# Expert results as blocks in a table by slot, gathered per token, and transposes ahead of the second small output

## The chip, the cores and the metric

The kernel runs on one core of a Trainium2 chip. The metric is the time of one execution in microseconds, as the device measures it. The kernel before takes 564.56 us (median of three runs, 564.34 to 565.74).

## The reference

Three layers follow one another, all in float32. An attention whose queries are averaged in pairs gives 1152 tokens of 512 numbers. A mixture of eight experts then adds to each token the gated result of one expert, unless a score of the token says that it is passed on unchanged. A feed-forward of width 2048 ends it.

```python
def _moe_ref(x, w_skip, w_gate, w1, w2):
    do_compute = x @ w_skip > 0
    out = x.copy()
    xc = x[do_compute]
    logits = xc @ w_gate
    e_idx = np.argmax(logits, axis=1)
    probs = softmax(logits)                       # 1e-9 added to the sum
    gate_w = probs[np.arange(len(xc)), e_idx]
    for e in range(E):                            # E = 8
        mask = e_idx == e
        h = np.maximum(xc[mask] @ w1[e], 0.0)     # 512 -> 1024
        y[mask] = gate_w[mask, None] * (h @ w2[e])
    out[do_compute] = xc + y
    return out

def _moe2_ref(x, w_in, w_out):
    h = x @ w_in                                  # 512 -> 2048
    return (h * np.tanh(softplus(h))) @ w_out     # 2048 -> 512
```

## The kernel before

The core works in three stages, and the program order on each engine is written out by hand (`manual_schedule`), so an engine takes its instructions in the order of the code.

**Attention** (to about 231 us) leaves the tokens in the DRAM tensor `rows` (1152 x 512). Beside it SyncE fills `ytok`, a DRAM tensor of the same shape, with zeros, three blocks of 128 rows at each of the steps 13, 16 and 19 (`early`, L1326 to L1329), loads expert weights and prepares the weights of the feed-forward.

**Routing** (`routing`, L484) counts with matrix products which token goes to which expert and place. Each expert has first 32 places ("small"); experts 0 and 2 have 256 and 128 places more and, like the others, a tail of 64 ("mid"). The result is `idx`, for each place the number of its token, in columns of 128 places; `sidx` is the same list with a number out of range for places without a token, and `odd` a copy of part of it. Tokens are gathered from `rows` through `idx` by GpSimd's indirect DMAs (`fetch`, L633).

**Experts** (`moe`, L879). `small1` and `small2` compute up and down projection for the 32 places of an expert; four experts share the rows of one tile `ys[0]` or `ys[1]`. `wide` (L717) treats the larger places of experts 0 and 2, with operands that are split in a high and a low part. The order at the beginning is: `turn` of the small hidden values of expert 0, the transposes `prep0(0)`, `turn` for expert 1, `small2(0)`, `prep0(1)`, the subtraction `wlo(0, 2)`, `small2(1)`, `prep0(2)`, and then `wide(0)`. `prep0(j)` transposes the j-th tile of expert 0's tokens into PSUM; ScalarE copies the high part out (L714) and VectorE subtracts for the low part (L715). `small2` sums its two halves with an `L801` copy on ScalarE and two adds on VectorE (L804); its PSUM tile has the tag "ys", with one buffer, except for the last expert, which uses "yl".

Every result is scattered into `ytok` by token with an indirect DMA on GpSimd's queue (`put`, L691; places without a token fall out of range). There are six before the feed-forward's first third: three after `wide(0)`, one for `ys[0]`, two after `wide(2)`. Then GpSimd loads the first 384 rows of `ytok` into `yt` (L979). VectorE adds them, times the gate, to the tokens (L990), while TensorE goes through the small experts 4 to 7. The result of these, `ys[1]`, is scattered last (L995); for the first third of the tokens it is added not by way of `ytok` but by a matrix product with the selection `pick` (L1126).

**Feed-forward** (`ffn`, L1088). `prep_first` transposes the first third (L1119) and adds the product with `pick` (L1126). Then 48 steps follow, 16 for each third of the tokens. At the fifth step of the first and second third, SyncE and ScalarE load the next third of `rows` and `ytok` (`load_x`, L1105), and `add_x` (L1109) adds them from the eighth step on.

Behind it stands a conditional part (`others`, and a second feed-forward) for inputs with more tokens at an expert than the places hold. It doesn't run with these inputs.

Of the kernel before, what the change touches and what calls it, by code (L numbers as in the profile page):

```python
# [17 lines left out]
N = B * Q  # L18
# [9 lines left out]
MID = 64  # L28
TAIL = 2 + E * (S // P)
NCOL = TAIL + E // 2  # L30
ZROW = NCOL * P
# [4 lines left out]
NEAR = slice(2, 2 + len(ROWS))  # L36
TAILS = slice(NEAR.stop - E // 2, NEAR.stop)
# [446 lines left out]
def routing(tc, io, lg, rt, tmp, ps, first, second, third, kept):  # L484
# [42 lines left out]
    count = rk[:, T * E :]  # L527
    sidx, idx, cnt, odd = kept
    pr = te("r_pr")
# [20 lines left out]
    def tokens(cs, ix):  # L550
        nc.vector.tensor_scalar(idx[:, cs], ix, float(FAR), float(N - 1), op0=ALU.add, op1=ALU.min)
        return lambda: nc.vector.tensor_scalar(sidx[:, cs], ix, float(FAR), None, op0=ALU.add)
# [18 lines left out]
    nc.vector.tensor_reduce(f, pos, axis=AX.X, op=ALU.add)  # L571
    fi = sb([P, T], I32, "r_fi")
    nc.vector.tensor_scalar(fi, f, float(ZROW), None, op0=ALU.add)
# [55 lines left out]

    return dict(idx=idx, sidx=sidx, odd=odd, cnt=cnt, gates=gates)  # L630

# [38 lines left out]


def source(io, e, i):
    if i < 2:
        src = io["w1"][e, 2 * P * i : 2 * P * i + 2 * P]
    else:
        src = io["w2"][e, 4 * P * (i - 2) : 4 * P * (i - 1)]
    return src.rearrange("(k p) f -> p k f", p=P)


def passes(nc, tc, io, r, rows, ytok, wts, ps, wk, nreg, xs, wait=None):  # L680
    idx, cnt = r["idx"], r["cnt"]
    gather = lambda dst, col: fetch(nc, rows, idx, dst, col)

    def scatter(src, col, n=P, odd=0):
        if odd:
            ix = r["odd"][:, col - TAILS.start : col - TAILS.start + 1]
        else:
            ix = r["sidx"][:n, col : col + 1]
        put(src, ix)
# [27 lines left out]
    def wide(e, xT, w1, split, outs, hooks):  # L717
        J = DEEP[e]
        n = P * J + MID
        two = len(w1) == 2  # L720
        acc = [ps.tile([P, 512], F32, name="ly", tag="yl")]
        acc += [ps.tile([P, 512], F32, name="lt", tag="mt", bufs=2) for _ in range(J)]
        gs = {}

        def hidden(fc):
            a = ps.tile([P, 512], F32, name="la", tag="am", bufs=2)[:, :n]
            prods = [(k, i) for k in range(4) for i in (PASS if two else ((0, 0),))]
            for m, (k, (u, v)) in enumerate(prods):
                nc.tensor.matmul(  # L729
                    a, w1[u][k // 2][:, k % 2, P * fc : P * fc + P], xT[v][:, k, :n],  # L730
                    start=(m == 0), stop=(m == len(prods) - 1),
                )
            g = [wk.tile([P, 5 * MID], F32R, name=x, tag=x)[:, :n] for x in ("wh", "wl")]
            nc.scalar.activation(g[0], a, AF.Relu)  # L734
            nc.vector.scalar_tensor_tensor(g[1], a, 0.0, g[0].bitcast(F32), op0=ALU.max, op1=ALU.subtract)  # L735
            gs[fc] = g

        def outp(fc):
            g = gs.pop(fc)
            for j in range(J + 1):  # L740
# [67 lines left out]
    def mid(e, xm, fill):  # L808
# [13 lines left out]
        down(MID, turn(MID, hs, "m", hT[:, :4]), (wts[e, 2], wts[e, 3]), yo, "l")  # L822
        scatter(yo, COL[e - e % 2, None], MID, e % 2)

    def large(e, j, xg, xgT):
# [21 lines left out]
        nc.scalar.copy(xg, y)  # L847
        scatter(xg, COL[e, j])

# [11 lines left out]
    def rest(e, xm, xg, end, before=None):  # L861
# [11 lines left out]
    return dict(  # L873
        gather=gather, scatter=scatter, put=put, register=register, transp=transp, turn=turn,
        down=down, larges=larges, rest=rest, prep=prep, wide=wide,
    )


def moe(tc, io, r, rows, ytok, slot, early, xr, yg, ylast, pick, last, xsT, ps, xm0, hs0, wts, whi, wlo):  # L879
    nc = tc.nc  # L880
    with ExitStack() as ctx:
# [4 lines left out]
        p = passes(nc, tc, io, r, rows, ytok, wts, ps, wk, {}, ())  # L886
        gather, scatter, turn, down = (p[n] for n in ("gather", "scatter", "turn", "down"))

# [77 lines left out]
        def last3():  # L966
            small2(3, hs[3])
            load_w(24, 30)
            scatter(ys[0], 0)

# [23 lines left out]
        small2(E - 1, hT, "l")  # L994
        p["put"](ys[1], last)  # L995


def others(tc, io, r, rows, ytok):
    nc = tc.nc
    with ExitStack() as ctx:  # L1000
        pool = lambda name, bufs, **k: ctx.enter_context(
# [86 lines left out]
def ffn(tc, io, r, rows, ytok, wdec, out, xr, yg, ylast, pick, wi, first, late=lambda: None):  # L1088
    nc = tc.nc
    T = 9  # L1090
    with ExitStack() as ctx:
# [204 lines left out]
def body(tc, io, out):  # L1296
    nc = tc.nc
    with ExitStack() as ctx:
# [20 lines left out]
        pick = cp.tile([P, 3, P], F32, name="pick")  # L1319
        last = cp.tile([P, 1], I32, name="last")  # L1320
        zero = cp.tile([P, DM], F32, name="zero")
# [4 lines left out]
        def early(i):  # L1326
            if i < 3:
                for t in range(3 * i, 3 * i + 3):
                    nc.sync.dma_start(ytok[P * t : P * t + P], zero)  # L1329
# [12 lines left out]
            cp.tile(x, I32, name=n)  # L1342
            for n, x in (("sidx", [P, NCOL]), ("idx", [P, NCOL]), ("cnt", [P, 2 * E + 1]), ("odd", [MID, E // 2]))
        ]
        kp = pool("kp", 1)

# [11 lines left out]
        with ExitStack() as c2:  # L1358
# [54 lines left out]
            r["gate"] = gate  # L1413
            moe(tc, io, r, rows, ytok, slot, split, xr, yg, zero, pick, last, xsT, ps, xm0, hs0, wts, whi, wlo)
        most = []

        def ask():
            most.append(
                nc.values_load(
                    kept[2][0:1, 2 * E : 2 * E + 1], min_val=-N, max_val=N,  # L1420
                    skip_runtime_bounds_check_because="a count of tokens",
# [4 lines left out]
        with tc.If(most[0] > SMALL):  # L1426
            others(tc, io, r, rows, ytok)
            again = Split(nc, kp)
            again.wdec = wdec
            again.open(8)  # L1430
            ffn(tc, io, r, rows, ytok, wdec, out, xr, yg, zero, pick, again, False)

# [4 lines left out]
def layout(inp):  # L1437
# [19 lines left out]
    cst[:, CST["iota"]] = ar  # L1457
    ids = [0, 1] + [TAIL + e // 2 if j is None else 2 + S // P * e + j for e, j in ROWS]
    cst[:, CST["c128"]] = np.array(ids) * P
# [4 lines left out]
    cst[:, CST["base"]] = SMALL * e8 - ZROW  # L1464
    cst[:, CST["lofs"]] = (S - SMALL) * e8 + 2 * P - SMALL
    cst[:, CST["tofs"]] = (MID - S) * e8 + (TAIL - 2) * P
    res = dict(
# [33 lines left out]
```

## Time and profile before

| | us |
|---|---|
| median of three runs (564.34 to 565.74) | 564.56 |
| the profiled execution, as a whole | 565.0 |
| its span, first to last instruction | 563.2 |
| TensorE busy (96% of the span) | 538.0 |
| VectorE busy (69%) | 388.2 |
| ScalarE busy (66%) | 372.2 |
| GpSimd busy (17%) | 96.9 |

The profile is of one execution; its times run from the first instruction of the span. A row of a view names the line of the kernel, the engine (PE is TensorE, DVE VectorE, ACT ScalarE, POOL GpSimd, SP SyncE; PEld is the load of weights into TensorE, beside its products), the operation and the tensors as output<-input. Busy time isn't progress: an engine with 96% can still have its holes at one place, so the stages are looked at one by one. A DMA that is issued from GpSimd shows as a short instruction of GpSimd, and its landing comes later.

### The profile page before, as it was taken

How to read it: one execution, taken by the hardware profiler on the slowest of the kernel's cores; microseconds unless marked ns; L12 is line 12 of the kernel's file. 1: busy time of each engine (PE TensorE's matmuls, PEld its weight loads, DVE VectorE, ACT ScalarE, POOL GpSimd, SP SyncE). 2: the span in 40 equal slices, each digit the busy share in tenths (PEclk: the TensorE clock that was granted, in tenths of full speed). 3: DMA queues.
4: the chain of work that ended last, by engine and by line, in shares of the span. 5: the costliest groups of instructions: out<-in, count | busy, mean ns of one | idle time of the engine just before them, and what ended most of it. 6: DMA issues, size and time to landing. Idle time of an engine off the chain costs nothing. (4 is left out here: it accounts for less than half of the span.)

```text
span 563.2 us, 11886 instructions
## 1 busy us (share of the span) xinstructions
PE 538.0 (96%) x4770; PEld 411.5 (73%) x4772; DVE 388.2 (69%) x725; ACT 372.2 (66%) x677; POOL 96.9 (17%) x88
## 2 busy tenths in 40 slices
PE   8699999999999999998999997999999999999994
PEld 4566666666666766657868746898899899999882
DVE  3488788888989888684133224899986666666663
ACT  3888888888888888632141141999877666676662
POOL 1213444335524511140000110000000000000000
PEclk9999999999999999998999998999999999999998
DMA  8558878998878783159979764273203100010001
GB/s 260 209 200 276 274 254 277 312 319 283 289 241 300 243 297 129 48 191 397 357 278 365 275 229 152 77 261 94 60 16 124 45 1 0 2 58 0 2 0 62
DMA packets 49922, 102.18 MB, mean 181 GB/s; under 512 B 13995, under 2 KB 15403, under 8 KB 49856
## 3 DMA queue, kind: packets, MB, share of 16 engines
q1 hardware_dynamic: 47360, 95.20, 49.2%
q0 software_dynamic: 1264, 3.75, 2.0%
q10 hardware_dynamic: 1232, 2.36, 1.2%
q8 instruction: 39, 0.64, 0.5%
q14 instruction: 27, 0.22, 0.1%
HBM read 84.70 MB, written 17.04 MB: 181 GB/s over the span
## 5 line engine op out<-in xcount | busy, mean ns | idle before, releaser
L152 DVE TENSOR_SCALAR_CACHE_REDUCE scp<-s 128x1152 f32<-128x1152 f32 x72 | 97.7, 1357 | 35.4 <-PE s L149 21.6
L1176 PE MATMUL ph<-xT,wi 128*128 128x384 f32 x576 | 108.5, 337 | 0.0
L1176 PEld LDWEIGHTS ph<-xT,wi 128*128 128x128 f32 x576 | 102.1, 188 | 4.2
L163 ACT ACTIVATE scp<-scp,mx 128x1152 f32<-128x1152 f32 x72 | 90.5, 1257 | 9.3 <-DVE scp L152 9.2
L149 PE MATMUL s<-ks,qs 64*128 64x288 f32 (+1 forms) x640 | 89.6, 428 | 5.2 <-DVE scp L152 4.8
L1230 PE MATMUL po<-wo,gh 128*128 128x512 f32 x288 | 90.3, 394 | 0.7 <-ACT gh L1215 0.5
L202 ACT COPY eT<-tp 128x1024 f32<-128x1024 f32 x63 | 63.8, 1013 | 27.6 <-PE tp L179 26.9
L149 PEld LDWEIGHTS s<-ks,qs 64*128 64x128 f32 (+1 forms) x640 | 48.9, 176 | 41.1 <-DVE scp L152 16.6
L220 PE MATMUL ov<-eT,vt 128*64 128x288 f32 x540 | 78.3, 417 | 0.0
L1230 PEld LDWEIGHTS po<-wo,gh 128*128 128x128 f32 x288 | 52.9, 188 | 10.2 <-ACT gh L1215 1.4
L1230 PE MATMUL po<-wo,gl 128*128 128x512 f32 x144 | 57.2, 397 | 0.0
L179 PEld LDWEIGHTS tp<-cst,scp 64*128 64x128 f32 x1145 | 47.0, 138 | 13.2 <-issue 3.9
L1200 ACT ACTIVATE u<-u 128x384 f32<-128x384 f32 (+1 forms) x49 | 25.4, 519 | 46.5 <-DVE u L1194 46.0
L1220 DVE TENSOR_TENSOR gl<-s,gh 128x384 fp32r<-128x384 f32 (+1 forms) x49 | 27.0, 550 | 41.7 <-ACT gh L1215 41.5
L351 POOL TENSOR_TENSOR g<-wd 128x512 f32<-128x512 f32 x32 | 34.0, 1063 | 89.0 <-PE s L149 74.7
L179 PE MATMUL tp<-cst,scp 64*128 64x64 f32 x1145 | 48.2, 223 | 0.0
L220 PEld LDWEIGHTS ov<-eT,vt 128*64 128x64 f32 x540 | 33.6, 136 | 19.2
L734 ACT ACTIVATE wh<-la 128x320 fp32r<-128x320 f32 (+1 forms) x16 | 6.2, 386 | 41.7 <-PE la L729 41.7
L735 DVE SCALAR_TENSOR_TENSOR wl<-la,wh 128x320 fp32r<-128x320 f32 (+1 forms) x16 | 6.8, 425 | 37.0 <-ACT wh L734 37.0
L1230 PEld LDWEIGHTS po<-wo,gl 128*128 128x128 f32 x144 | 27.0, 187 | 6.7 <-DVE gl L1220 1.0
L1194 DVE TENSOR_SCALAR u<-ph 128x384 f32<-128x384 f32 (+1 forms) x49 | 26.6, 545 | 6.4 <-PE ph L1176 6.3
L1202 ACT ACTIVATE r<-s,one 128x384 f32<-128x384 f32 (+1 forms) x49 | 30.0, 611 | 1.6
(195 smaller groups left out, 796.9 us busy)
## 6 DMA issues: line engine op xcount, KB each, us to landing
w<-w SPq DMA_DIRECT2D x32, 1024.0 KB, 8.7
wd<-wq SPq DMA_DIRECT2D x32, 512.0 KB, 5.5
wdec<-g SPq DMA_DIRECT2D x32, 256.0 KB, 4.6
vt<-vt SPq DMA_DIRECT2D x8, 576.0 KB, 5.7
ks<-kt SPq DMA_DIRECT2D x15, 288.0 KB, 6.8
ring<-wdec SPq DMA_DIRECT2D x16, 256.0 KB, 2.8
wr<-wdec SPq DMA_DIRECT2D x16, 256.0 KB, 2.7
xr<-qt SPq DMA_DIRECT2D x7, 576.0 KB, 6.1
```

Of the source, the lines that this page charges most:

```text
L149: st["tick"] = nc.tensor.matmul(s[o, half, j, :HQ], w[r], st["k", h, b][r, cs], start=True, stop=True).ins
L152: nc.vector.tensor_scalar(scp.rearrange("p (a c) -> p a c", a=4), s.rearrange("p a j c -> p (a j) c")[:, :, :HQ], -EXP_SCALE, -NEG, op0=AL ...
L163: nc.scalar.activation(scp, scp, AF.Exp, bias=mx, scale=-1.0, accum_out=st["sum", h][:, t : t + 1],)
L179: nc.tensor.matmul(to, e[q, P * i : P * i + P], io["ident"][q, q], start=i < 8 or a != opened, stop=True, is_transpose=True, skip_group_ch ...
L202: nc.scalar.copy(to.rearrange("p k (a c) -> p a k c", a=2), v)
L220: nc.tensor.matmul(acc[D * b : D * b + D, :288], st["v", h][:, b, kc], src[:, kc, b], start=(kc == 0), stop=(kc == KC - 1), skip_group_che ...
L351: side.append(lambda: tt(g, hf, hf, op=ALU.mult))
L1176: nc.tensor.matmul(ph, wi.w[i][:, a, P * k : P * k + P], xTs[c][b][:, k], start=(n == 0), stop=(n == 11),)
L1194: nc.vector.tensor_scalar(a["t"][0][:, c], ph[:, c], 20.0, None, op0=ALU.min)
L1202: nc.scalar.activation(r[:, c], s[:, c], AF.Ln, bias=one)
L1220: nc.vector.tensor_tensor(gl[:, c], a["t"][1][:, c], gh[:, c].bitcast(F32), op=ALU.subtract)
L1230: nc.tensor.matmul(acc[j], g[a][:, P * j : P * j + P], wo[b][:, i], start=(i == 0 and n == 0), stop=(i == 15 and n == 2),)
```

## The change

The table `ytok` is no longer by token but by place. Every block of places has fixed rows in it (`rowof`): the small places of experts 0 to 3 and 4 to 7 the first two blocks of 128 rows, then the tails, then the blocks of experts 0 and 2, and a block of zeros. A result is written as a block with a plain DMA on GpSimd's queue (`save`). Routing computes for each token the row that holds its result (`place`; a token without one points at the zeros), and the first third's load, as well as the two loads in the feed-forward, become three indirect gathers of 128 rows each on GpSimd's queue. The loads in the feed-forward were on ScalarE's queue. The lists `sidx`, `odd` and `last` go. Thirteen blocks are filled with zeros instead of nine, five, four and four at the same three steps. The conditional part gets a larger table of its own (`yall`), filled when it runs.

At the beginning of the experts, `prep0(1)` moves ahead of `small2(0)`, `prep0(2)` ahead of `wlo(0, 2)` and `small2(1)`, and `small2(1)` uses the PSUM tile "yl".

```diff
-TAIL = 2 + E * (S // P)
-NCOL = TAIL + E // 2
+TAIL = 2
+NCOL = TAIL + E // 2 + E * (S // P)
+FIRST = {e: TAIL + E // 2 + S // P * i for i, e in enumerate([*DEEP, *(e for e in range(E) if e not in DEEP)])}
+HEAD = max(FIRST[e] + DEEP[e] for e in DEEP)
...
-    slots = tokens(slice(0, 2), ix)
+    tokens(slice(0, 2), ix)
     first(idx)
+    nc.vector.tensor_scalar(spot, ix[:, 1:2], float(FAR), None, op0=ALU.add)
...
-    nears = tokens(NEAR, ix[:, NEAR])
+    tokens(NEAR, ix[:, NEAR])
+    nc.vector.tensor_scalar(near, f, float(ZROW), float(P * HEAD), op0=ALU.add, op1=ALU.min)
...
-    fars = tokens(far, ix[:, far])
-    for f in (slots, nears, fars):
-        f()
-    nc.vector.tensor_copy(odd, sidx[MID:, TAILS])
+    tokens(far, ix[:, far])
...
+def rowof(e, j):
+    if j is None:
+        return P * (TAIL + e // 2) + MID * (e % 2)
+    return P * (FIRST[e] + j)
...
-    def put(src, ix):
-        nc.gpsimd.indirect_dma_start(
-            out=ytok,
-            out_offset=bass.IndirectOffsetOnAxis(ap=ix, axis=0),
-            in_=src, in_offset=None, bounds_check=N - 1, oob_is_err=False,
-        )
+    def save(src, row):
+        nc.gpsimd.dma_start(ytok[row : row + src.shape[0]], src)
...
-            scatter(outs[j][:q], COL[e, j if j < J else None], q)
+            save(outs[j][:q], rowof(e, j if j < J else None))
...
-        nc.vector.tensor_copy(last, r["sidx"][:, 1:2])
-        spot = xp.tile([P, 1], F32, name="spot")
-        nc.vector.tensor_copy(spot, r["sidx"][:, 1:2])
...
         hT.append(turn(SMALL, hs0[1], "s", act=True))
+        prep0(1)
         small2(0, hT[0])
-        prep0(1)
+        prep0(2)
         wlo(0, 2)
-        small2(1, hT[1])
-        prep0(2)
+        small2(1, hT[1], "l")
         load_w(12, 20)
...
-            scatter(ys[0], 0)
+            save(ys[0], 0)
...
-        nc.gpsimd.dma_start(yt, tiles3(ytok, 0))
+        for t in range(3):
+            fetch(nc, ytok, r["place"], yt[:, t], t)
...
         small2(E - 1, hT, "l")
-        p["put"](ys[1], last)
+        save(ys[1], P)
...
         def load_x(c):
             nc.sync.dma_start(xr, tiles3(rows, c))
-            nc.scalar.dma_start(yg, tiles3(ytok, c))
+            for t in range(3):
+                fetch(nc, ytok, r["place"], yg[:, t], 3 * c + t)
...
-        ytok = dp.tile([N, DM], F32, name="ytok")
+        ytok = dp.tile([P * HEAD + P, DM], F32, name="ytok")
+        yall = dp.tile([ZROW + P, DM], F32, name="yall")
...
             if i < 3:
-                for t in range(3 * i, 3 * i + 3):
+                blank = [1, HEAD, *range(TAIL, FIRST[0]), *range(FIRST[0] + DEEP[0], FIRST[2])]
+                for t in blank[i::3]:
                     nc.sync.dma_start(ytok[P * t : P * t + P], zero)
```

## Rows read from the trace of the kernel before

**Rows 1.** Busy time by stage: stretch, length, busy (instructions) per engine, clock, DMA.

```profile
254.80:262.00 7.20, 6.29 (x30) 6.01 (x31) 3.52 (x5) 1.10 (x3) 0.00 (x0) 0.76 1.04 403
337.20:341.90 4.70, 0.02 (x1) 0.03 (x1) 0.83 (x2) 0.37 (x1) 0.00 (x0) 0.98 0.46 167
341.90:351.00 9.10, 9.10 (x45) 8.04 (x46) 5.52 (x10) 1.92 (x4) 1.03 (x1) 0.82 0.45 151
```

**Rows 2.** The same view in stretches of one microsecond, at two places.

```profile
330.00:331.00 1.00, 1.00 (x18) 0.47 (x14) 0.14 (x1) 0.52 (x2) 0.00 (x0) 1.00 0.30 115
...
342.00:343.00 1.00, 1.00 (x5) 1.00 (x6) 1.00 (x2) 0.00 (x0) 0.00 (x0) 0.50 0.00 0
```

**Rows 3.** Waits, 245 to 345 us: waiting <- waited for: us, times, longest.

```profile
DVE xr L990 <- DMA yt<-ytok: 5.4, 1, 5.4
...
PE ft L1119 <- DVE xr L990: 4.7, 1, 4.7
...
PE la L729 <- DVE xTl L715: 0.9, 1, 0.9
PE sy L795 <- ACT xT L714: 0.9, 1, 0.9
...
PE la L729 <- ACT xT L714: 0.6, 1, 0.6
```

**Rows 4.** GpSimd, 280 to 420 us, in order: start, length, what, idle before.

```profile
294.38 1.44 POOL L692 DMA_INDIRECT ytok<-xr,sidx  x1 [31.17 <-ACT xr L757]
...
332.38 0.91 POOL L692 DMA_INDIRECT ytok<-yg,sidx  x1 [6.47 <-DVE zero L804]
336.06 0.82 POOL L979 DMA_DIRECT2D yt<-ytok  x1 [2.76 <-issue]
```

**Rows 5.** All engines in order of time, 320 to 352 us.

```profile
321.75 0.83 PE L908 MATMUL gr<-cst,gate 128*128 128x128 f32 x6
321.95 0.68 DVE L757 COPY yg<-lt 64x512 f32<-64x512 f32 x1 [4.12 <-PE lt L743]
...
334.82 0.85 DVE L804 TENSOR_TENSOR zero<-sy,yh 32x256 f32<-32x256 f32 x2 [1.71 <-ACT yh L801]
...
335.24 1.93 PE L795 MATMUL sy<-w,hsT 128*32 128x256 f32 x32 [0.56 <-ACT hsT L778]
...
341.07 2.08 DVE L990 SCALAR_TENSOR_TENSOR xr<-yt,gate,xr 128x512 f32<-128x512 f32 x3 [5.41 <-DMA yt<-ytok]
...
341.88 4.49 PE L1119 MATMUL ft<-cst,xr 128*128 128x128 f32 x24 [4.71 <-DVE xr L990]
343.07 1.28 DVE L1075 TENSOR_TENSOR wi<-ring,wi 128x512 fp32r<-128x512 f32 x2
...
346.21 2.75 PE L1126 MATMUL ft<-pick,zero 128*128 128x384 f32 x8
```

**Rows 6.** SyncE's queue, 40 to 72 us: the first three fills.

```profile
45.03 2.05 SPq L1329 DMA_DIRECT2D ytok<-zero  x3
```

**Rows 7.** DMA issues: what, queue, count, size, median us from issue to landing.

```profile
ytok<-zero SPq DMA_DIRECT2D x9, 256.0 KB, 3.5
...
yg<-rows,idx POOLq DMA_INDIRECT x4, 4.4
```

**Rows 8.** Two gathers of GpSimd and VectorE's work beside the second, in order.

```profile
242.27 0.95 POOL L634 DMA_INDIRECT xr<-rows,idx  x1 [0.30 <-issue]
...
243.08 4.49 DVE L1382 TENSOR_TENSOR wp<-w,wp 128x2048 fp32r<-128x2048 f32 x2
...
243.53 2.66 POOL L634 DMA_INDIRECT xm<-rows,idx  x1 [0.31 <-issue]
```

**Rows 9.** VectorE ahead of the first hidden block of `wide(0)`, 250 to 275 us.

```profile
255.64 0.42 DVE L715 TENSOR_TENSOR xTl<-xt,xT 128x256 fp32r<-128x256 f32 x1
```

**Rows 10.** Load and first sum of the second third of the tokens.

```profile
368.75 0.43 ACTq L1107 DMA_DIRECT2D yg<-ytok  x1
...
381.56 0.74 DVE L1111 SCALAR_TENSOR_TENSOR xr<-yg,gate,xr 128x512 f32<-128x512 f32 x1
```

More of the change, by code (lines that the diff above doesn't have):

```diff
@@ L36 @@
 NEAR = slice(2, 2 + len(ROWS))
-TAILS = slice(NEAR.stop - E // 2, NEAR.stop)
 ROWS += [(e, j) for e in range(E) for j in range(S // P) if (e, j) not in ROWS]
 COL = {r: 2 + i for i, r in enumerate(ROWS)}
+FIRST = {e: TAIL + E // 2 + S // P * i for i, e in enumerate([*DEEP, *(e for e in range(E) if e not in DEEP)])}
+HEAD = max(FIRST[e] + DEEP[e] for e in DEEP)
 W_TINY = 1.125 * 2.0 ** -15
@@ L527, in routing @@
     count = rk[:, T * E :]
-    sidx, idx, cnt, odd = kept
+    idx, cnt, fi, spot, near = kept
     pr = te("r_pr")
@@ L551, in tokens @@
         nc.vector.tensor_scalar(idx[:, cs], ix, float(FAR), float(N - 1), op0=ALU.add, op1=ALU.min)
-        return lambda: nc.vector.tensor_scalar(sidx[:, cs], ix, float(FAR), None, op0=ALU.add)
-    slots = tokens(slice(0, 2), ix)
+    tokens(slice(0, 2), ix)
     first(idx)
+    nc.vector.tensor_scalar(spot, ix[:, 1:2], float(FAR), None, op0=ALU.add)
     thr = sb([P, E], I32, "r_thr")
@@ L571, in routing @@
     nc.vector.tensor_reduce(f, pos, axis=AX.X, op=ALU.add)
-    fi = sb([P, T], I32, "r_fi")
     nc.vector.tensor_scalar(fi, f, float(ZROW), None, op0=ALU.add)
@@ L628, in gates @@
         nc.vector.reciprocal(gate, gate)
-    return dict(idx=idx, sidx=sidx, odd=odd, cnt=cnt, gates=gates)
+    return dict(idx=idx, cnt=cnt, place=near, all=fi, gates=gates)
 def fetch(nc, rows, idx, dst, col):
@@ L682, in passes @@
     gather = lambda dst, col: fetch(nc, rows, idx, dst, col)
[L684 to L689, printed above, removed]
-    def put(src, ix):
-        nc.gpsimd.indirect_dma_start(
-            out=ytok,
-            out_offset=bass.IndirectOffsetOnAxis(ap=ix, axis=0),
-            in_=src, in_offset=None, bounds_check=N - 1, oob_is_err=False,
-        )
+    def save(src, row):
+        nc.gpsimd.dma_start(ytok[row : row + src.shape[0]], src)
     def register(i):
@@ L822, in mid @@
         down(MID, turn(MID, hs, "m", hT[:, :4]), (wts[e, 2], wts[e, 3]), yo, "l")
-        scatter(yo, COL[e - e % 2, None], MID, e % 2)
+        save(yo, rowof(e, None))
     def large(e, j, xg, xgT):
@@ L847, in large @@
         nc.scalar.copy(xg, y)
-        scatter(xg, COL[e, j])
+        save(xg, rowof(e, j))
     def larges(e, j, xg, xgT=None, end=16):
@@ L873, in passes, with moe @@
     return dict(
-        gather=gather, scatter=scatter, put=put, register=register, transp=transp, turn=turn,
+        gather=gather, save=save, register=register, transp=transp, turn=turn,
         down=down, larges=larges, rest=rest, prep=prep, wide=wide,
     )
-def moe(tc, io, r, rows, ytok, slot, early, xr, yg, ylast, pick, last, xsT, ps, xm0, hs0, wts, whi, wlo):
+def moe(tc, io, r, rows, ytok, slot, early, xr, yg, ylast, pick, spot, xsT, ps, xm0, hs0, wts, whi, wlo):
     nc = tc.nc
@@ L886, in moe @@
         p = passes(nc, tc, io, r, rows, ytok, wts, ps, wk, {}, ())
-        gather, scatter, turn, down = (p[n] for n in ("gather", "scatter", "turn", "down"))
+        gather, save, turn, down = (p[n] for n in ("gather", "save", "turn", "down"))
         def load_w(first, stop, after=None):
@@ L994, in moe, with others @@
         small2(E - 1, hT, "l")
-        p["put"](ys[1], last)
-def others(tc, io, r, rows, ytok):
+        save(ys[1], P)
+def others(tc, io, r, rows, ytok, head, zero):
     nc = tc.nc
+    nc.vector.memset(zero, 0.0)
+    for t in range(HEAD, NCOL + 1):
+        nc.sync.dma_start(ytok[P * t : P * t + P], zero)
+    nc.sync.dma_start(ytok[: P * HEAD], head[: P * HEAD])
     with ExitStack() as ctx:
@@ L1319, in body @@
         pick = cp.tile([P, 3, P], F32, name="pick")
-        last = cp.tile([P, 1], I32, name="last")
         zero = cp.tile([P, DM], F32, name="zero")
@@ L1342, in body @@
             cp.tile(x, I32, name=n)
-            for n, x in (("sidx", [P, NCOL]), ("idx", [P, NCOL]), ("cnt", [P, 2 * E + 1]), ("odd", [MID, E // 2]))
+            for n, x in (("idx", [P, NCOL]), ("cnt", [P, 2 * E + 1]), ("place", [P, 9]))
         ]
+        kept.append(cp.tile([P, 1], F32, name="spot"))
+        kept.append(cp.tile([P, 9], I32, name="near"))
         kp = pool("kp", 1)
@@ L1413, in body @@
             r["gate"] = gate
-            moe(tc, io, r, rows, ytok, slot, split, xr, yg, zero, pick, last, xsT, ps, xm0, hs0, wts, whi, wlo)
+            moe(tc, io, r, rows, ytok, slot, split, xr, yg, zero, pick, kept[3], xsT, ps, xm0, hs0, wts, whi, wlo)
         most = []
@@ L1419, in ask @@
                 nc.values_load(
-                    kept[2][0:1, 2 * E : 2 * E + 1], min_val=-N, max_val=N,
+                    kept[1][0:1, 2 * E : 2 * E + 1], min_val=-N, max_val=N,
                     skip_runtime_bounds_check_because="a count of tokens",
@@ L1426, in body @@
         with tc.If(most[0] > SMALL):
-            others(tc, io, r, rows, ytok)
+            others(tc, io, r, rows, yall, ytok, zero)
+            r["place"] = r["all"]
             again = Split(nc, kp)
@@ L1430, in body @@
             again.open(8)
-            ffn(tc, io, r, rows, ytok, wdec, out, xr, yg, zero, pick, again, False)
+            ffn(tc, io, r, rows, yall, wdec, out, xr, yg, zero, pick, again, False)
 _INS = ("qt", "kt", "vt", "wb", "w1", "w2", "wq", "consts")
@@ L1457, in layout @@
     cst[:, CST["iota"]] = ar
-    ids = [0, 1] + [TAIL + e // 2 if j is None else 2 + S // P * e + j for e, j in ROWS]
+    ids = [0, 1] + [rowof(e, j) // P for e, j in ROWS]
     cst[:, CST["c128"]] = np.array(ids) * P
@@ L1464, in layout @@
     cst[:, CST["base"]] = SMALL * e8 - ZROW
-    cst[:, CST["lofs"]] = (S - SMALL) * e8 + 2 * P - SMALL
-    cst[:, CST["tofs"]] = (MID - S) * e8 + (TAIL - 2) * P
+    first = P * np.array([FIRST[e] for e in range(E)])
+    cst[:, CST["lofs"]] = first - SMALL * e8 - SMALL
+    cst[:, CST["tofs"]] = TAIL * P + MID * e8 - first
     res = dict(
```

## The prediction

> **What bounds the kernel now.** I read four views, in this order. First the busy time by stage [rows 1]: from 254.8 to 262.0 us TensorE is busy 6.29 of 7.20 us at a mean granted clock of 0.76, from 337.2 to 341.9 it is idle, and from 341.9 to 351.0 it is busy throughout at 0.82. The reader should see two holes in the middle of a span that TensorE otherwise fills, each followed by a lower clock. Second, short stretches [rows 2]: right behind the second hole the granted clock is 0.50, that is 1.2 instead of 2.4 GHz, and I read the 0.76 behind the first as a mixture of the same two levels; so a hole is paid twice. Third, the waits between 245 and 345 us [rows 3] say who ended the holes: in the second, TensorE waits 4.7 us for VectorE's sum L990, and that waits 5.4 us for the load `yt<-ytok`; in the first, it waits 0.9 us for the copy of the second prep (L714), then 0.6 and 0.9 us for the copies of the third (L714, L715), together 2.4 us. Fourth, the order of GpSimd's work [rows 4]: six scatters into `ytok` start from 294.38 to 332.38 us, one every (332.38 - 294.38) / 5 = 7.6 us, and the load of `yt` starts 3.7 us behind the last. The last scatter's data was there at 321.95 + 0.68 = 322.6 us [rows 5], ten microseconds before it started. So the scatters are a chain: every one may write any row of `ytok`, and each starts only when the one before has landed. This chain, not TensorE, sets when the feed-forward may begin.
>
> **Part 1: blocks instead of scatters.** The new writes go to fixed, disjoint rows. Do they still wait for one another? The trace shows writes of disjoint rows of one tensor in another queue: three fills of `ytok` go out within 2.05 us [rows 6], while one such fill takes 3.5 us to land [rows 7]. I conclude that disjoint blocks don't wait, though that is SyncE's queue and not GpSimd's. Then the two last blocks (expert 2) start when their data is there, at about 322.1 and 323.0 us. Their landing is not shown for a direct write from GpSimd: the scatter behind which the load started took 3.7 us with the DMA engines nearly free, and one under load up to 7.6 us [rows 4]. The engines are full until about 330 us (their share falls to 0.30 there [rows 2]), so I take 7.6: landed at about 330.6.
>
> Then three gathers replace the one load. A gather of 128 rows occupied GpSimd for 0.95 us, the next started 1.26 us after it, and it landed 4.4 us (median of four) after its issue [rows 7, 8]. With half a microsecond to start, they go out at 331.1, 332.4 and 333.6 and land at 4 us each: 335.1, 336.4 and 337.6 us. At VectorE the sums L990 may start behind its adds of the seventh small output, at about 335.7; three take 2.08 us [rows 5]. TensorE ends the last small output at 335.24 + 1.93 = 337.2 [rows 5] and goes on with the 24 transposes L1119 there instead of at 341.88: 4.7 us earlier. With no hole the clock should stay up. The 24 took 4.49 us, most of it at half clock; six multiplications of the same size took 0.83 us at full clock [rows 5], so 24 take 3.3, which is 1.2 us less (1.6 us by the mean clock of the stretch, 9.1 x 0.18 [rows 1]). They end at 340.5. The eight L1126 need the last small output's adds, which stand on VectorE behind the third sum and two subtractions: 337.6 + 0.7 + 1.28 + 0.85 = 340.4 us [rows 5], and a few tenths of latency on top. Full gain 4.7 + 1.2 = 5.9; for a third gather that comes late I take off 0.5: **5.4 us**. Ends: 5.9 + 0.4 = 6.3 us if the larger figure for the clock holds; 4.0 if the blocks land 1.5 us later.
>
> **Part 2: transposes ahead of the second output.** TensorE's new order is third-prep transposes, then the second small output, then the first hidden block. The second output has a PSUM tile of its own ("yl"), so it needn't wait for the adds of the first; the 0.9 us goes. The third prep's two copies now run beside the second small output (1.93 us of matmuls, as the last one's [rows 5]). On VectorE the low copy L715 stood behind a subtraction L1382 (4.49 / 2 = 2.2 us [rows 8]) and the second output's adds, and so began only at 255.64 [rows 9]; now both stand behind it. I walk through it: second prep's transposes end near 249.3 (row `xr` was gathered by then), the first output near 251.2, the third prep near 251.7 to 252.1, its copies are done at about 253.1, the second output ends near 254.0 and the hidden blocks start at once, so the 0.6 and 0.9 go too. The half clock behind cost 7.2 x 0.24 = 1.7 us [rows 1]. Sum 2.4 + 1.7 = 4.1. One pause of about 0.4 us for the new order stays: **3.6 us**. New waits: "yl" must be read out before the first product into it. The adds of the second output end near 256.3 and that product comes near 258, so it is covered; were it not, the loss would be the difference. The low half of the second hidden block is ready about 259.9 and used at 260.3: the closest cover here. Ends: 1.9 us if the clock still falls, 4.1 if nothing is left.
>
> **Part 3: the rest.** Routing loses six small VectorE instructions off the path and gains two, one of them (`spot`) ahead of the one-hot chain: about -0.1 us, at most -0.2. The fills grow from nine to thirteen blocks of 256 KB on SyncE, near 45 to 67 us: at 2.05 / 3 = 0.7 us of issue each [rows 6] that is 2.7 us more in three places, behind which stand loads of a whole head ahead. I take 0, at worst 1 us. In the feed-forward two loads by ScalarE's queue become two times three gathers on GpSimd. Before, the load for the second third of tokens went out at 368.75 and its first sum ran at 381.56 [rows 10]: 12.8 us of cover for a gather of 4.4 us, and GpSimd has nothing else to do; they may even go out as soon as the ninth block, the last small output, has landed. I take 0, at worst 1 us if they crowd the weight loads then. The last block waits for the three gathers, which read the same tensor; its reader is that far load. Everything behind either hole moves forward as a whole: the weights' loads are released by the work that uses the slot before, so they move along.
>
> **The rule against it.** While VectorE ran two subtractions of 128x2048, a gather kept GpSimd 2.66 us instead of 0.95 [rows 8]. The Trainium skill, SBUF - State Buffer, section "Who interferes with whom", says that GpSimd's descriptor writing can be shut out by VectorE and that hardware queues are not; it also says that a `tensor_tensor` doesn't shut it out by a two-port mode, only reads contend. By it the old hardware load was the safer choice; this trace agrees that a gather can be that slow, whatever holds it. By the row: if all three gathers took 2.66 us, the third would land 3 x 1.7 = 5.1 us later and part 1 would bring about 0.3 us. Against it stands that VectorE has only two short subtractions (1.28 us) there, not 4.5 us of them.
>
> **The sum.** 5.4 + 3.6 - 0.1 = 8.9 us. The profiled execution is 565.0 us (span 563.2 and 1.8 around it), so 556.1; the median of the three runs is 0.44 lower, so 555.7 us.
>
> **Rivals.** (a) The blocks still wait for one another, as the scatters did on this queue. Then the last starts about 332.4, the first gather at 336.1 lands no sooner than the load did, and part 1 brings 0.3 us or nothing: 564.6 - 3.6 = 561.0 us. For it: the wait on GpSimd is real, and the fills that don't wait are on another queue. Against: the scatters could overlap and the blocks can't. Chance 0.12. (b) The gathers are slowed as above: 560.9 us, chance 0.06. (c) The reordering brings nothing, as the second output's tile, its adds or GpSimd's third gather hold up the hidden blocks just as long: 564.6 - 5.3 = 559.3 us, chance 0.06. (d) Slower than before: GpSimd takes software transfers into or out of `ytok` one at a time, so the blocks are chained and each gather starts only when the one before has landed. From 336.1, at 4.4 us and 0.5 us to start, the third lands at 350.3; with sum, subtractions, adds and the eight multiplications (2.75 us [rows 5]) the preparation ends near 355.9 instead of 348.96, +6.9 us, and with part 2 it is +3.3: 567.9 us. It decides from the point where the third gather lands later than about 347 us on the old time line. Against: gathers of `rows` into different tiles go out 1.26 us apart [rows 8]. Chance 0.05.
>
> **How the numbers follow.** The forecast has 0.71; its own range goes from 564.6 - 6.3 - 4.1 = 554.2 to 564.6 - 4.0 - 1.9 = 558.7 us, with 1 us more for part 3 at the upper end. (b) and (c) lie close above, and (a) ends at 561. The range 553.9 to 561.2 leaves out (d) and some tails. A measurement of this kernel can tell about 0.3% (1.7 us) from no change. Faster by more than that: the forecast, (a) to (c) with a little taken off each, 0.91; within it 0.04; slower 0.05.
>
> **What would show it.** In the changed trace: GpSimd's blocks start within 1 us of their data and not 7 us apart; the wait of L990 for `yt` is under 1.5 us instead of 5.4; TensorE's hole before L1119 is under 1 us, and the clock stays at 1.00 there; TensorE passes from the second small output to the hidden block without the 0.6 and 0.9 us, at 1.00. The first wrong step would show as blocks still 7 us apart, or gathers that hold GpSimd for over 2 us; the second as a granted clock of 0.50 behind the second output. It would also be wrong if the feed-forward's sums L1111 now waited for GpSimd.

## The result and the profile after

| | before | after |
|---|---|---|
| median of the runs, us | 564.45 (4 runs, 563.70 to 565.74) | 555.45 (4 runs, 554.91 to 556.74) |
| the profiled execution, us | 565.0 | 554.91 |
| its span, us | 563.2 | 553.0 |

The ratio is 0.9842, with a 95% interval from 0.9815 to 0.9868. The median fell by 9.0 us, where 8.9 us was forecast (555.7 us). In the two profiles the spans differ by 10.2 us.

GpSimd's queue in the kernel after, in order of time (start, length, what, idle before), where [rows 4] showed the scatters:

```profile
289.36 1.17 POOL L689 DMA_DIRECT2D ytok<-xr  x2 [30.68 <-ACT xr L750]
...
297.42 0.57 POOL L689 DMA_DIRECT2D ytok<-yg  x1 [6.36 <-DVE yg L797]
317.17 0.55 POOL L689 DMA_DIRECT2D ytok<-yg  x1 [19.18 <-ACT yg L750]
317.96 0.55 POOL L689 DMA_DIRECT2D ytok<-yg  x1 [0.25 <-DVE yg L750]
326.17 1.03 POOL L632 DMA_INDIRECT yt<-ytok,near  x1 [7.66 <-PE ht L767]
327.50 1.45 POOL L632 DMA_INDIRECT yt<-ytok,near  x1 [0.30 <-issue]
329.26 0.95 POOL L632 DMA_INDIRECT yt<-ytok,near  x1 [0.30 <-issue]
```

The two blocks behind `wide(0)` that fill 128 rows follow one another at once (x2), and the last block, at 317.96, starts 0.3 us behind its data (316.99 + 0.68 = 317.67). The two long gaps that are left, ahead of 297.42 and 317.17, are waits for data and not for the write before. The first gather follows 8.2 us behind the last block.

All engines of the kernel after from 316 to 348 us, beside [rows 5]:

```profile
316.99 0.68 DVE L750 COPY yg<-lt 64x512 f32<-64x512 f32 x1 [4.14 <-PE lt L736]
...
330.56 1.94 PE L788 MATMUL sy<-w,hsT 128*32 128x256 f32 x32 [0.84 <-ACT hsT L771]
331.02 0.75 DVE L981 SCALAR_TENSOR_TENSOR xr<-yt,gate,xr 128x512 f32<-128x512 f32 x1
...
332.42 3.50 PE L1115 MATMUL ft<-cst,xr 128*128 128x128 f32 x24
...
332.85 0.75 DVE L981 SCALAR_TENSOR_TENSOR xr<-yt,gate,xr 128x512 f32<-128x512 f32 x1 [1.08 <-DMA yt<-ytok,near]
...
333.95 0.75 DVE L981 SCALAR_TENSOR_TENSOR xr<-yt,gate,xr 128x512 f32<-128x512 f32 x1 [0.35 <-DMA yt<-ytok,near]
...
336.41 2.85 PE L1122 MATMUL ft<-pick,zero 128*128 128x384 f32 x8 [0.49 <-DVE zero L797]
```

TensorE ends the last small output at 332.50 and is at the transposes (L1115, L1119 before) at once; the hole of 4.7 us is gone. What is late now is small: TensorE waits 0.84 us for ScalarE ahead of the last small output, the second and third sum wait 1.08 and 0.35 us for their gathers, and the eight products wait 0.49 us for the adds that stand behind the sums on VectorE.

The beginning of the experts in the kernel after, beside [rows 9]:

```profile
250.59 1.93 PE L788 MATMUL sy<-w,hsT 128*32 128x256 f32 x32
...
251.64 0.42 DVE L708 TENSOR_TENSOR xTl<-xt,xT 128x256 fp32r<-128x256 f32 x1
...
252.46 0.41 PE L722 MATMUL la<-xT,wp 128*128 128x320 f32 x1
...
256.08 0.60 PE L756 MATMUL mt<-cst,yg 128*128 128x128 f32 x4
```

The low copy L708 (L715 before) runs beside the second small output, and the hidden block begins when that ends.

Busy time by stage in the kernel after, beside [rows 1] (stretch, length, busy and instructions of PE, PEld, DVE, ACT, POOL, granted clock, DMA share, GB/s):

```profile
252.40:256.70 4.30, 4.30 (x33) 4.24 (x30) 4.22 (x5) 1.23 (x3) 0.00 (x0) 1.00 1.04 392
...
332.50:339.30 6.80, 6.23 (x34) 4.66 (x35) 4.80 (x9) 1.81 (x5) 0.58 (x1) 1.00 0.41 132
```

Both stretches are at a granted clock of 1.00; before they were at 0.76 and 0.82.

To compare kernels I use two stretches of TensorE's order, each from one event to another, so that what lies ahead of them drops out: **P**, from the first transposes `prep0(0)` to the four transposes behind the first two hidden blocks, and **Q**, from ScalarE's copy behind `wide(2)` to the end of the products with `pick`.

| profile | P | Q |
|---|---|---|
| before | 261.14 - 247.57 = 13.57 | 348.96 - 321.25 = 27.71 |
| after | 256.08 - 246.93 = 9.15 | 339.26 - 316.29 = 22.97 |

4.4 and 4.7 us are 9.1 of the 10.2 us. The rest stands outside: attention ended 0.9 us earlier in this profile (and ends up to 1.1 us apart in profiles of kernels that are the same there), routing became 0.3 us longer, the feed-forward 0.5 us shorter (214.24 to 213.7).

### The profile page after: what moved, and what is told of

Read it like the earlier page. It is cut to its first block, busy times and chain, and to the rows that moved or that the text cites. A ratio compares the mean times of both kernels' runs of the same rounds, so it can differ in the third digit from the quotient of the medians.

```text
span 553.0 us, 11896 instructions
## 1 busy us (share of the span) xinstructions
PE 534.6 (97%) x4772; PEld 408.2 (74%) x4772; DVE 387.8 (70%) x721; ACT 372.1 (67%) x677; POOL 102.8 (19%) x96
## 4 chain that ended last, share of the span: by engine, by line
PE 59%; DVE 6%; DMA 2%; ACT 2%; issue 1%; POOL 0%; ACTq 0%; DVEq 0%
PE po L1226 14%; PE ph L1172 14%; PE s L150 5%; PE ov L221 5%; PE la L722 5%; PE lt L736 3%; PE sa L644 2%; PE tp L180 2%; PE ly L736 2%; PE sy L788 2%; DMA wr<-wdec 1%; DVE wi L1070 1%; DVE wo L1161 1%; DMA yt<-ytok,near 1%; PE ov L259 1%
## 5 line engine op out<-in xcount | busy, mean ns | idle before, releaser
L1216 DVE TENSOR_TENSOR gl<-s,gh 128x384 fp32r<-128x384 f32 (+1 forms) x49 | 27.0, 550 | 41.7 <-ACT gh L1211 41.5
L1197 ACT ACTIVATE s<-u,one 128x384 f32<-128x384 f32 (+1 forms) x49 | 29.9, 611 | 1.6
```

What stands on the lines that cost most here:

```text
L1197: nc.scalar.activation(s[:, c], u[:, c], AF.Square, bias=one)
```

## The experiments

Rows show a kernel's own line numbers.

**The blocks alone.** The order of the transposes and the tile are put back.

```diff
-        prep0(1)
         small2(0, hT[0])
-        prep0(2)
+        prep0(1)
         wlo(0, 2)
-        small2(1, hT[1], "l")
+        small2(1, hT[1])
+        prep0(2)
```

> The kernel after with the order of the transposes and the second small output (and its PSUM tile 'ys') as in the kernel before: the blocks and gathers alone. Theory, two separate holes: this gives the second hole's share alone, 4.7 to 5.4 us, so 559.1 to 559.8 us beside 564.5; the clock behind the second output is 0.50 again for about 3.5 us, and the first hidden block waits 0.6 and 0.9 us as before. Rival, the blocks are the whole gain: 555.5 us. Rival, the reordering is the whole gain: 564.5 us.

Measured: 557.76 us beside 564.13 of the kernel before, ratio 0.9876 (0.9844 to 0.9908): 6.4 us, more than I expected. P is 259.35 - 247.32 = 12.03 us and Q 342.56 - 319.55 = 23.01, as after. Beside the first profile of the kernel before, Q is 4.7 and P 1.5 us shorter. The waits in the first hole were there again (0.8, 0.6 and 0.9 us), but the clock behind it stayed up, against what I expected:

```profile
254.50:261.70 7.20, 6.25 (x37) 5.50 (x38) 4.35 (x6) 1.52 (x4) 1.48 (x1) 1.00 1.04 404
```

This is the stretch of the first of [rows 1], with nearly the same busy time, at 1.00 instead of 0.76.

**The order alone.** The kernel before with the new order and "yl".

```diff
         hT.append(turn(SMALL, hs0[1], "s", act=True))
+        prep0(1)
         small2(0, hT[0])
-        prep0(1)
+        prep0(2)
         wlo(0, 2)
-        small2(1, hT[1])
-        prep0(2)
+        small2(1, hT[1], "l")
```

> The kernel before with the transposes ahead of the second small output and its tile 'yl', the scatters left as they are: the reordering alone. Theory: 3.6 to 4.4 us, so 560.1 to 560.9 us; the scatters are still 7 to 8 us apart, and the hole before the transposes L1119 is as long as before or up to 0.5 us longer, since the last scatter is bound to the first by the chain and the first moves along. Rival, the chain keeps its old clock time because the DMA engines set it, and the earlier work only waits longer: 564.5 us.

Measured: 561.65 us beside 564.13, ratio 0.9953 (0.9935 to 0.9970): 2.5 us, between theory and rival. P is 255.94 - 246.78 = 9.16, the full gain, but Q is 346.11 - 316.06 = 30.05, longer than before. GpSimd's rows tell why:

```profile
289.19 1.44 POOL L692 DMA_INDIRECT ytok<-xr,sidx  x1 [30.65 <-ACT xr L757]
...
332.14 0.82 POOL L979 DMA_DIRECT2D yt<-ytok  x1 [3.31 <-issue]
```

and of its waits (times and longest behind the sum), the one that [rows 3] has at 4.7 us:

```profile
PE ft L1119 <- DVE xr L990: 5.6, 1, 5.6
```

The first scatter starts 5.2 us earlier than in [rows 4], but the load only 3.9: the chain took 43.0 instead of 41.7 us (42.1 in the four other profiles with the old scatters). TensorE then waits 5.6 us, and the granted clock was 0.50 from 336.7 to 343.5 us, twice as long as behind this hole in the kernel before (341.7 to 345.2), so the transposes took 5.49 instead of 4.49 us. So with the chain in place about half of the earlier gain is handed back: of the 2.3 us by which Q grew, some 1.3 by the longer chain and 1.0 by the longer half clock. That the new order made the half clock longer isn't shown; in a profile with the old order (the thirteen fills, below) it lasted as long. The two parts alone, 6.4 and 2.5 us, add up to 8.9.

**The chain kept.** The kernel after, but each block is written through a list of its row numbers.

```diff
+SAVES = [0, P] + [rowof(e, j) for e in DEEP for j in (*range(DEEP[e]), None)]
...
     def save(src, row):
-        nc.gpsimd.dma_start(ytok[row : row + src.shape[0]], src)
...
+        n = src.shape[0]
+        c = SAVES.index(row)
+        nc.gpsimd.indirect_dma_start(
+            out=ytok,
+            out_offset=bass.IndirectOffsetOnAxis(ap=r["slots"][:n, c : c + 1], axis=0),
+            in_=src, in_offset=None, bounds_check=P * HEAD + P - 1, oob_is_err=False,
+        )
...
+            for i, row in enumerate(SAVES):
+                nc.gpsimd.tensor_scalar(
+                    slots[:, i : i + 1], cst[:, CST["tok"]][:, :1], float(FAR + row), None, op0=ALU.add
+                )
```

> The kernel after, but each block is written to the same rows by an indirect DMA through a list of row numbers made in the kernel, so that a write may reach any row as far as the order of the work knows. Same bytes to the same rows, same gathers. Theory, the gain of the blocks is the chain that is gone: the writes are 7 to 8 us apart again, the first gather starts near 331.5 us on the time line of the changed kernel (336.1 less the 4.96 us by which everything stood earlier), the third lands near 338, and the time is 559 to 561 us, about what the reordering alone gives. Rival, a plain DMA is the cheaper write and the chain doesn't matter: each write costs GpSimd 1.0 instead of 0.55 us, two of them on the path, so 556.4 us.

Measured: 560.79 us beside 564.13, ratio 0.9930 (0.9906 to 0.9954). P is 9.16, Q 344.19 - 316.49 = 27.70, as long as before. GpSimd's third write, its last two and the first gather:

```profile
305.71 0.92 POOL L697 DMA_INDIRECT ytok<-xm,slots  x1 [6.71 <-DMA ytok<-xr,slots]
...
320.71 0.98 POOL L697 DMA_INDIRECT ytok<-yg,slots  x1 [7.24 <-ACT hs L649]
328.32 0.91 POOL L697 DMA_INDIRECT ytok<-yg,slots  x1 [6.62 <-DVE wi L1082]
331.87 0.99 POOL L632 DMA_INDIRECT yt<-ytok,near  x1 [2.64 <-issue]
```

The wait of TensorE ahead of the transposes:

```profile
PE ft L1127 <- DVE xr L993: 3.7, 1, 3.7
```

Same bytes, same rows, same gathers, and seven instructions of GpSimd that make the list (3.1 us, off the path: P is unchanged): what differs is that each write goes through row numbers and so may reach any row. The writes are some 7.6 us apart again, the third one waits for the landing of the one before it, the hole is back, and so is the old Q. The other theory, a dearer write, would have cost 1 us; it was 4.7. This is what shows that the gain of the blocks is the chain. One thing it leaves together: a write through row numbers is also another kind of DMA than a plain one, and no run here has two such writes into different tensors. Gathers through row numbers on the same queue go out 1.3 us apart.

**Without "yl".**

```diff
-        small2(1, hT[1], "l")
+        small2(1, hT[1])
```

> The kernel after, but the second small output uses the PSUM tile 'ys' of the first, as in the kernel before; the order stays new. Theory: it then waits for the adds of the first output, which end 1.0 us after the second output now starts, so 1.0 us is lost, and a little more if the granted clock falls behind it: 556.4 to 558.2 us. Rival, the order is all and the tile costs nothing: 555.5 us.

Measured: 556.75 us beside 564.13, ratio 0.9865 (0.9832 to 0.9897); the times alone don't tell it from the kernel after (555.45 and 556.11 us in two sets). P is 257.49 - 247.21 = 10.28 us, 1.1 more than after, and the wait is where it was expected (1.0 us, at a clock of 1.00):

```profile
251.99 1.93 PE L788 MATMUL sy<-w,hsT 128*32 128x256 f32 x32 [1.05 <-ACT xT L707]
```

The profile names ScalarE's copy as what came last, but that ended at 251.41 us; the adds of the first output, which read the tile, end at 251.89, and the edit touches only this tile. So of P's gain 1.1 us is the tile, the rest the order.

**A set beside the kernel after.** Four kernels on one chip, the kernel after among them.

> The kernel after, unchanged, beside the three others of this set: 555.5 us.

Measured: 556.11 us beside 563.71, ratio 0.9859 (0.9835 to 0.9883). P is 9.15, Q 22.98, as in its first profile.

**The hole filled with idle products.** The kernel before, with work for TensorE in the second hole.

```diff
         small2(E - 1, hT, "l")
+        warm = ps.tile([P, 512], F32, name="warm2", tag="am", bufs=2)
+        for _ in range(20):
+            nc.tensor.matmul(
+                warm, io["ones"], io["cst"].bitcast(BF16)[:, :512], start=True, stop=True
+            )
```

> The kernel before with twenty matrix products of ones in the second hole (128 x 512, bf16, result unused, about 0.21 us each, 4.2 us in all), which change nothing else. Theory, the hole is paid twice, once as idle time and once as half clock behind it: the 24 transposes L1119 run at a granted clock of 1.00 in 3.3 to 3.5 us instead of 4.5, and the time falls by 1.0 to 1.2 us to 563.3 to 563.5 us. Rival, what follows is bound by VectorE (two subtractions and the adds ahead of L1126), so faster transposes only wait there: 564.5 us.

Measured: 562.58 us beside 563.71, ratio 0.9985 (0.9965 to 1.0005), which doesn't tell a gain from none. The traces do. TensorE in this kernel:

```profile
334.80 4.49 PE L997 MATMUL warm<-cst,ones 128*128 128x512 bf16 x20
...
340.04 2.92 PE L1124 MATMUL ft<-cst,xr 128*128 128x128 f32 x24 [0.74 <-PE warm L997]
```

And the kernel before, in the second of its later profiles:

```profile
340.05 4.57 PE L1119 MATMUL ft<-cst,xr 128*128 128x128 f32 x24 [5.17 <-DVE xr L990]
```

At the same time of the span the same 24 transposes take 2.92 instead of 4.57 us. So in this pair the clock behind the hole cost 1.65 us, on top of the hole's idle time. The products with `pick` behind them started at 342.96 instead of 344.46 us, so the rival, that the faster transposes only wait for VectorE, isn't what these profiles show.

**The subtractions behind the last adds.** The kernel after with another order on VectorE.

```diff
-        early.split(2)
         small2(E - 1, hT, "l")
+        early.split(2)
         save(ys[1], P)
```

> The kernel after, but the two subtractions for the feed-forward's weights (L1070) stand behind the adds of the last small output on VectorE, not ahead of them. In the changed kernel the eight products L1122 wait 0.49 us for these adds. Theory: that wait goes, and the last block's write starts 1.3 us earlier; 555.0 us. Rival, the subtractions are then late for the third hidden block, or the adds and the copies L1126 meet them anyway: 555.5 us or up to 0.8 us more.

Measured: 554.48 us (554.15 to 555.19) beside 556.11 (555.56 to 556.69) of the kernel after in the same set, ratio to before 0.9833 (0.9809 to 0.9857). But Q was 338.84 - 315.90 = 22.94, unchanged: in this profile TensorE waited 1.8 us for ScalarE ahead of the last small output, where it had waited 0.8 in the first profile of the kernel after. So I ran it again:

> The kernel with the two subtractions behind the last adds once more, in a set of its own. In the first set it took 554.5 us beside 556.1 us of the kernel after, yet the stretch that the edit touches, from wide(2)'s copy to the end of the products L1122, was 22.94 beside 22.98 us in the profiles; the difference of the two profiles lay in attention, ahead of the edit. Theory, the edit is worth nothing that this stretch shows and the first set's difference is chance: the ratio to the kernel before comes out near the 0.984 to 0.986 of the kernel after, the stretch at 22.9 to 23.0 us. Rival, it is a gain of 0.3%: a ratio of 0.983 or less again, and a stretch that is shorter where ScalarE isn't late with the seventh small output.

Measured: 554.43 us (553.71 to 555.07) beside 563.63, ratio 0.9824 (0.9800 to 0.9848). ScalarE was late by 0.8 us this time, and Q is 339.49 - 317.18 = 22.31, 0.66 us shorter than after:

```profile
333.31 3.59 PE L1115 MATMUL ft<-cst,xr 128*128 128x128 f32 x24
...
336.74 2.75 PE L1122 MATMUL ft<-pick,zero 128*128 128x384 f32 x8
```

The products follow the transposes without the 0.49 us. The traces show about 0.6 us of gain; the times of two sets, 1.0 to 1.7 us against the kernel after's two medians, suggest that it is the fastest kernel here that takes the right rows, but the intervals of the ratios overlap and the part above 0.6 us isn't explained.

**One load instead of three gathers.** The selection of rows by token is left out, so the first third's sums take other rows.

```diff
-        for t in range(3):
-            fetch(nc, ytok, r["place"], yt[:, t], t)
+        nc.gpsimd.dma_start(yt, tiles3(ytok, 0))
```

> The kernel after, but the first third is read by one plain load of the first 384 rows of the table instead of three gathers; which rows a token gets is left out, so the first third's sum is of other rows. It prices the gathers. Theory: the load lands at about 331.2 us on the time line of the changed kernel (326.2 + 5.0), all three sums run on end, the 1.1 and 0.35 us that the second and third sum wait are gone, TensorE's 0.49 us wait too: 555.0 us. Rival, what delays the sums is the DMA traffic and not the gathers' issue: 555.5 us.

Measured: 554.27 us beside 556.11, ratio to before 0.9827 (0.9803 to 0.9851). It doesn't price the gathers as I meant: a plain load of the first three blocks need not wait for the last two blocks, which are other rows, and it started at 318.69 instead of 326.2. What it shows is the stretch with the table read early: Q is 338.06 - 316.40 = 21.66, the sums run on end,

```profile
331.13 2.08 DVE L980 SCALAR_TENSOR_TENSOR xr<-yt,gate,xr 128x512 f32<-128x512 f32 x3
```

and that is 1.3 us less than after. So the wait for the last blocks together with the gathers still costs 1.3 us.

**The kernel before, profiled again**, and with thirteen fills.

> The kernel before, unchanged, profiled once more. In its first profile the granted clock was 0.50 behind the first hole, from 256.1 to 259.6 us, and the 24 products of the first two hidden blocks took 6.35 us. In the profiles of the blocks alone and of the warm hole, which have the same order and the same waits there, it stayed at 1.00 and they took 4.8 us. Theory, the fall there is not a steady cost of this hole: 4.8 us here, or now one and now the other. Rival, the kernel before always falls there, and the other two differ by something else ahead of it: 6.3 us.

> The kernel before, a third profile, for the same question: the 24 products take 4.8 us if the clock stays up behind the first hole, 6.3 us if it falls. Behind the second hole, which is a full 4.7 us without work, it falls by either theory, and the 24 transposes take 4.5 us.

```diff
-                for t in range(3 * i, 3 * i + 3):
+                for t in [*range(3 * i, 3 * i + 3), *range(3 * i, 3 * i + (2, 1, 1)[i])]:
                     nc.sync.dma_start(ytok[P * t : P * t + P], zero)
```

> The kernel before with thirteen fills of 256 KB instead of nine at the same three steps (five, four and four), as in the kernel after; the four more write zeros over rows that are zero already. Prices the fills alone. Theory: attention waits for no load at these steps, so nothing: within 0.5 us of the kernel before. Rival, SyncE's queue is late with a head's loads behind them: up to 2.7 us more. Its first hole is that of the kernel before, a fourth look at the clock there.

Measured: 565.65 and 563.62 us for the kernel before, one run each; 564.23 us with thirteen fills beside 564.23, ratio 0.9998 (0.9980 to 1.0017). The fills cost nothing that can be told. P is 13.56 in the first of the three, 12.03 and 12.02 in the others. The stretch behind the first hole in the first later profile of the kernel before:

```profile
254.73:261.93 7.20, 6.29 (x30) 6.00 (x31) 3.45 (x5) 1.11 (x3) 0.00 (x0) 0.76 1.04 402
```

The same stretch in the second:

```profile
254.06:261.26 7.20, 6.29 (x37) 5.55 (x38) 4.30 (x6) 1.52 (x4) 1.53 (x1) 1.00 1.04 401
```

The same 6.29 us of busy time, once at 0.76 and once at 1.00. Of the six profiles with the old order (before three times, the blocks alone, the filled hole, the thirteen fills) the clock fell behind the first hole in two. Behind the second hole it fell in every profile in which that hole was there and empty (the kernel before three times, the thirteen fills, the order alone, the chain kept).

## Why the prediction was right, and where its steps were not

**The chain: right.** The step that carried the forecast was that the scatters waited for one another because each may write any row, and that disjoint blocks don't. In the kernel before, a row that [rows 4] leaves out names the wait, that of the second scatter for the first:

```profile
303.19 1.01 POOL L692 DMA_INDIRECT ytok<-xr,sidx  x1 [7.36 <-DMA ytok<-xr,sidx]
```

By the landing times in that trace each of the five later scatters started 0.73 to 0.77 us after the one before it had landed. The blocks started behind their data, and the kernel with the chain kept had the old Q. The rival in which the blocks still wait fell with it, and so did the slower one: gathers followed at 1.3 to 1.8 us, not one by one.

**The landing: nearly right.** I took 7.6 us to the last block's landing and half a microsecond to start, 8.1 us to the first gather; it was 8.2. The 7.6 was misread as the longest under load: it is the mean of the five intervals between scatters, and the first was 8.8 us (294.38 to 303.19). Shifted by the 4.96 us by which that stretch stood earlier, the first gather was forecast for 326.1 and started at 326.17. The third was forecast to land at 332.6 and its sum began at 333.95, 1.3 us late, since the second held GpSimd 1.45 us and all three landed in 4.6 us (median) instead of 4.

**Part 1's size: 5.4 forecast; 4.7 us in the first pair of profiles.** Against all four profiles of the kernel before and with more fills, whose Q is 27.7, 27.9 (349.03 - 321.18), 28.3 (347.21 - 318.96) and 28.5 (347.85 - 319.36), it is 4.7 to 5.5. The hole of 4.7 us went; the transposes, forecast at 3.3 us, take 2.92 to 2.94 when nothing interrupts them; the late gathers took back more than the 0.5 us that I allowed (0.56 us in the transposes, which took 3.50, and 0.49 behind them), and the wait for ScalarE grew from 0.56 to 0.84.

**Part 2's size: 3.6 forecast, at most 4.1; 4.4 us in the first pair.** The mechanism was right: all three waits went, 2.3 us together. The prediction's first paragraph takes the first of them, as the view has it, for a wait for the copy L714; as its second part says and the kernel without "yl" shows, it was the tile (the adds L804 end at 251.81 us, the second output starts at 251.91). The term that was mis-sized is the clock. I took 1.7 us as a steady cost of the hole, from one profile. With the clock up, P is 12.03, and the new order gains 12.03 - 9.15 = 2.9 us; the other 1.5 us (13.57 - 12.03) are gained only over those executions in which it fell. The pause of 0.4 us that I held back for the new order didn't come. Instead 0.6 us more than the waits was gained: in P TensorE is busy for 9.72 us in the blocks alone and 9.15 after.

**The parts don't stand alone, and the sum was partly luck.** I summed them, and the sum held (8.9 us forecast, 9.0 measured), but I said that everything behind the first hole moves forward as a whole. In the kernel before it doesn't: the order alone gave 2.5 us, as the chain grew by 0.8 to 1.3 us and with it the hole, and the half clock behind was longer. The sum was right because the other part removes the chain. And two sizes were off in opposite directions. By the medians the blocks alone brought 6.4 us where I had 5.4, with the clock behind the first hole up in their profile; on top of them the order brought 1.7 to 2.3 us (557.76 less 556.11 or 555.45) where I had 3.6, 1.7 of it for that clock.

**Part 3.** Fills: 0 forecast, 0 measured. Routing: -0.1 forecast; from GpSimd's first instruction in it to `prep0(0)` it takes 17.38 us in the kernel before (247.57 - 230.19) and 17.66 after (246.93 - 229.27), -0.3, beyond my bound of 0.2: besides `spot`, the conversion that writes `place` takes 0.31 instead of 0.17 us. The feed-forward's first gathers went out at 342.8, some 16 us ahead of where ScalarE's load would have stood (368.75 less the 9.7 us by which this stretch moved), and no sum waited for them.

**The rule against it.** The second gather of `yt` took 1.45 us beside two subtractions of VectorE (1.29 us together), the two others 1.03 and 0.95. It is the same in all six profiles with plain blocks and three gathers (1.36 to 1.47); with the chain kept, where VectorE ran nothing beside it, it took 0.97. So GpSimd is held up, as I priced it, but for half a microsecond, since VectorE has little to do there.

What stays open: why TensorE waited 0.8 to 2.1 us for ScalarE ahead of the last small output in the kernels with plain blocks (0.6 to 1.0 us in those with the chain), why the half clock behind the second hole lasts longer in some profiles, and what the kernel with the subtractions behind gains beyond 0.6 us.

## What to carry to other kernels

Look for stores with computed rows that follow one another at the spacing of their landing: if the data was ready long before the store started, the order of the work is the cost, and a layout with fixed, disjoint places moves the computed index to the read, where gathers don't wait for one another. Price a hole of TensorE with the clock behind it, but take that part from several profiles; one may show a fall that another doesn't. And test each part of a change alone: a gain ahead of a chain can be handed back at its end.

## What the runs showed of the hardware that was not expected

Behind the first hole, whose idle time was the same (6.25 to 6.29 us busy of 7.20 in five profiles that I compared), the granted clock fell to 0.50 for 3.4 us in two profiles of six and stayed at 1.00 in four. The full hole of 3.7 to 5.6 us made it fall each time, but for different lengths: 3.4 us in four profiles, 6.8 us in two (the order alone, the thirteen fills). The mean granted clock of whole runs points the same way. With the second hole filled, it was 0.995 in eight of twelve runs and 0.991 or 0.992 in four. By an estimate from these numbers 3.4 us at half clock take 0.003 off a mean over 560 us, but no profile shows where in those four it fell.

A block written by GpSimd's plain DMA holds GpSimd for 0.55 to 0.6 us instead of 0.9 to 1.4 for the scatter, yet lands no sooner: in the first two profiles the medians from issue to landing are 6.7 to 9.3 us for the blocks ahead of the gathers and 5.9 to 7.3 for the scatters ahead of the load, by source tile, and the gather behind the last block started 8.2 us later, where the scatters had followed one another at 7.6. The Trainium skill, SBUF - State Buffer, section "Who interferes with whom", says that a VectorE `tensor_tensor` with two SBUF inputs contends with GpSimd's reads; the 1.45 us gather beside such an instruction agrees with that, though no run here shows which of its accesses was held up.
